# Reading q and the block decays as 32x32 blocks turned by VectorE, and loading v amid a unit's block steps, in a gated linear attention and mixture-of-experts kernel

## The chip, the cores and the metric

The kernel runs on one core of a Trainium2 chip. The metric is device time in microseconds, the median of several runs; lower is better. One further execution was recorded by the hardware profiler.

## The reference

A gated linear attention over 4 batches of 8 heads, 768 tokens and head size 48 is followed by a mixture of 8 experts with a dense, Sinkhorn-normalised routing:

```python
for t in range(S):
    state = alpha[:, :, t, :, None] * state + np.einsum('bhd,bhe->bhde', k[:, :, t], v[:, :, t])
    y[:, :, t] = np.einsum('bhd,bhde->bhe', q[:, :, t], state)
x = y.transpose(0, 2, 1, 3).reshape(3072, 384)
P = np.exp(x @ w_gate - max)
for _ in range(8):
    P /= P.sum(1, keepdims=True) + 1e-9
    P /= P.sum(0, keepdims=True) + 1e-9
    P *= N / E
out = sum(P[:, e:e+1] * (np.maximum(x @ w1[e], 0) @ w2[e]) for e in range(8))
```

## The kernel before, in words

The program has two halves. In the first, up to about 700 us, the attention is computed while TensorE (PE) is filled up with tiles of the first three experts (`moe_tile`; their products stand under the names `ps<-xT,w` and `ps<-w,h`). In the second the other five experts run alone. The change touches the first half only.

The 3072 tokens are cut into 12 units of 256 tokens (4 batches of 3), each of two chunks of 128. Units 0 and 1 go through `direct_chunk`. Units 2 to 11 go through the **block path**. `attn_block` (line 484) works in a layout with a block of 16 tokens of one head on each partition: it loads q, alpha and k into the single-buffered tiles qt, al and kt (line 493), takes products on GpSimd (POOL) and their sums and decays on VectorE (DVE), and at its end writes the decayed k and q, the products of the decays and the block matrix to DRAM scratch (ks, qs, ds, dsw, As; lines 572 to 579). It then reads them back in the token-on-partition layout (KN, QN, DN, an, and VN straight from the input; lines 580 to 587), and reads a window of decays (win, line 592). All of these transfers are issued by SyncE (SP), one after the other, in the order of the code. TAB is 3: from unit 3 on the state uses the table made from win, and k128 is None.

`attn_decays` (line 598) turns the sixteen block decays DN on PE (four transposes into psd, line 604), and DVE copies them to dT. `attn_chunk` (line 641) turns k and q of a chunk on PE: four 128x128 transposes each into psk and psq (line 652), copied to Tk and Tq by ScalarE (ACT, line 654). DVE makes the decayed halves from them (decq, deck). PE then forms psl, psy and the state.

The order of the work is written by hand in the strings START and UNIT (lines 40 and 41): b is a block step, c a chunk step, d the decays, f a piece of an expert tile, a capital lets POOL take the loads. `run` (line 911) obeys them and puts off a step that `early_` holds to be too early. On every engine the instructions then stand in that order, and an instruction that waits holds up all that stands behind it on its engine. An expert tile uses one of four PSUM banks; ACT writes its relu, and DVE the remainder (`h<-ps,h`, line 245), before the bank is free for the fourth tile after it.

```python
for x, y in ((qt, q), (al, alpha), (kt, k)):
    (GE if lop[0] else SP).dma_start(x, src(y))
```

From unit 6 on these three loads are issued by SP right behind the win loads of the unit before; those of units 3 to 5 are issued by POOL.

Of the kernel before, what the change touches and what calls it, by code (L numbers as in the profile page):

```python
# [9 lines left out]
F32 = mybir.dt.float32  # L10
# [15 lines left out]
def tile_gla_moe(ctx: ExitStack, tc: tile.TileContext, q, k, v, alpha, wg, w1, w2, out):  # L26
# [42 lines left out]
    def tr(out_, in_, idn):  # L69
        tc.keep_in_program_order(nc.tensor.transpose(out=out_, in_=in_, identity=idn))  # L70
# [82 lines left out]
    def quarter(j):  # L153
        return slice(32 * j, 32 * j + 32)
# [132 lines left out]

    QN = [ap1.tile([P, NCH, H, DP], F32, name=f"QN{i}") for i in range(2)]
    KN = [ap1.tile([P, NCH, H, DP], F32, name=f"KN{i}") for i in range(2)]
    DN = [ap1.tile([16, H, DP], F32, name="DN")] * 2  # L290
    VW = DP + D
    ST = [ap1.tile([P, NP, 2 * D], F32, name=f"ST{i}") for i in range(2)]
    VN = [ap1.tile([P, NCH, NP, VW], F32, name=f"VN{i}") for i in range(2)]
# [3 lines left out]
    PRE, SUF, Q32, K32 = ([ap1.tile([P, NCH, NP, 2, n], F32, name=f"{x}_{i}") for i in range(2)]  # L297
                          for x, n in (("pre", 4), ("suf", 4), ("q32", 2), ("k32", 2)))

    for x in DN[:1] + ST:  # L300
        GE.memset(x, 0.0)
    for x in PRE + SUF + Q32 + K32:
        GE.memset(x, 1.0)
# [24 lines left out]
    for i in range(NLV):  # L328
        L = 1 << i

        r = sm.tile([P, 16], F32, tag="oddr", name=f"oddr_{i}")
        VE.tensor_reduce(r[:, :16 // L], same.rearrange("p (n z t) -> p n z t", z=2, t=L)[:, :, 0],
                         axis=AX.X, op=ALU.add)
        VE.tensor_copy(odd[:, i].rearrange("p (n t) -> p n t", t=L),
                       r[:, :16 // L].unsqueeze(2).to_broadcast([P, 16 // L, L]))

    def load_v(x, b, t0, Q=SP):
        for r in range(2):
# [145 lines left out]
    def attn_block(b, u, got):  # L484
# [6 lines left out]
        qt, kt, al = (ap1.tile([P, 16, D], F32, tag=x, name=f"{x}_{nm}") for x in ("qt", "kt", "al"))  # L491
        for x, y in ((qt, q), (al, alpha), (kt, k)):
            (GE if lop[0] else SP).dma_start(x, src(y))
        if TAB <= g < TAB + 2:
            SP.dma_start(dsw[g % 2][:, :, 8:].rearrange("h c n d -> (h c) n d"),
                         ones[:2 * H, None, :D].to_broadcast([2 * H, 7, D]))
# [11 lines left out]
        def total(o, t):  # L508
            vec.tensor_reduce(o, t, axis=AX.X, op=ALU.add)
# [35 lines left out]
        if True:  # L545

            t = mult(pool, "tmp4", [16], Af[:, 0:256:17], qt, kt)
            yield
            total(*t)
            yield  # L550
            vec.tensor_mul(qt, qt, al)
            for L in (1, 2, 4, 8):
                todo, merge = level(L)
                for x in todo:
                    t = mult(pool if lop[0] else x[0], *x[1:])
                    yield
                    total(*t)
                    if L == 8:
                        yield
                merge()  # L560
            yield
# [2 lines left out]
        ks = dr.tile([H, U, D], F32, tag="ks", name=f"ks_{nm}")  # L564
        ds = dr.tile([H, 16, D], F32, tag="ds", name=f"ds_{nm}")
        As = dr.tile([H, U, 16], F32, tag="As", name=f"As_{nm}")
        qn, kn, dn = QN[g % 2], KN[g % 2], DN[g % 2]
        vn = VN[g % 2]
        an = ap2.tile([P, NCH, H, 16], F32, tag="an", name=f"an_{nm}")
        def put(t, t_):  # L570
            for x, y in ((ks, ko), (qs, qo)):
                dma(x[:, t:t_].rearrange("h (n t) d -> n h (t d)", t=16), y[t // 2:t_ // 2])

        put(0, U)
        dma(ds.rearrange("h n d -> n h d"), al[:, 0])
        for c in range(NCH) if g >= TAB else ():
            dma(dsw[g % 2][:, c, :8].rearrange("h n d -> n h d"), al[c * 64:c * 64 + 64, 0])
        if True:
            dma(As.rearrange("h (n s) t -> n h (s t)", s=16), Af)
        for c in range(NCH):  # L580
            sl = slice(c * P, (c + 1) * P)
            dma(kn[:, c, :, :D], ks[:, sl].rearrange("h t d -> t h d"))
            dma(qn[:, c, :, :D], qs[:, sl].rearrange("h t d -> t h d"))
            if c == 0:
                dma(dn[:, :, :D], ds.rearrange("h n d -> n h d"))
            dma(an[:, c], As[:, sl].rearrange("h p t -> p h t"))
            load_v(vn[:, c], b, t0 + c * P)
        if g >= TAB:
            win = ap1.tile([P, 7, D], F32, tag="tmp2", name=f"win_{nm}")
# [2 lines left out]
                dma(win[c * 64:c * 64 + 64], bass.AP(tensor=e.tensor, offset=e.offset,  # L592
                                                     ap=[[D, 8], [NCH * 15 * D, H], [1, 7 * D]]))
            got["win"] = win
        got.update(qn=qn, kn=kn, dn=dn, vn=vn, an=an)
        yield

    def attn_decays(b, u, got):

        nm = f"{b}_{u}"  # L600
        dn = got["dn"]
        psd = psa.tile([P, 512], F32, tag="psa", name=f"psd_{nm}")
        for j in range(NP):
            tr(psd[:, j * 16:(j + 1) * 16], dn[:, 2 * j:2 * j + 2].rearrange("p h d -> p (h d)"), ident[:16, :16])
        dT = ap2.tile([P, NCH, NP, 2, 4], F32, tag="dT", name=f"dT_{nm}")
        VE.tensor_copy(dT.rearrange("p c j z n -> p c j (z n)"),
                              psd[:, :NP * 16].rearrange("p (j c n) -> p c j n", c=NCH, n=8))

        g2 = (b * NU + u) % 2
        pre, suf, q32, k32 = PRE[g2], SUF[g2], Q32[g2], K32[g2]  # L610
# [30 lines left out]
    def attn_chunk(b, ch, got):  # L641
# [4 lines left out]
        tt = b * (S // P) + ch  # L646
        nm = f"{b}_{ch}"
        T2 = []
        for s in "kq":
            ps = psa.tile([P, 512], F32, tag="psa", name=f"ps{s}_{nm}")  # L650
            for j in range(NP):
                tr(ps[:, j * P:(j + 1) * P], got[s + "n"][:, c, 2 * j:2 * j + 2].rearrange("p h d -> p (h d)"), ident)
            t = ap2.tile([P, NP, P], F32, tag=f"T{s}", name=f"T{s}_{nm}")
            SE.copy(t.rearrange("p j t -> p (j t)"), ps)
            T2.append(t)
# [18 lines left out]
        for L, tq, tk in ((32, got["q32"][:, c].rearrange("p j z b -> p (j z) b"),  # L674
# [5 lines left out]
        GE.tensor_mul(A.rearrange("p h (n t) -> p n h t", t=16),  # L680
                             got["an"][:, c].unsqueeze(1).to_broadcast([P, 8, H, 16]),
                             mask.unsqueeze(2).unsqueeze(3).to_broadcast([P, 8, H, 16]))
        tabbed = got["k128"] is None
        kb = None
        if tabbed and not c:
            win = got["win"]
# [820 lines left out]
```

## Time and profile before

| | us |
|---|---|
| median of 3 runs (1647.58 to 1651.91) | 1651.86 |
| the profiled execution, its own time | 1645.72 |
| its span, first to last instruction | 1643.8 |
| PE busy | 1591.0 (97%) |
| DVE busy | 1262.3 (77%) |
| ACT busy | 916.5 (56%) |
| POOL busy | 390.9 (24%) |

The busy time of an engine is given with its share of the span. Matmuls are pipelined, so that a busy PE need not be at its peak; what a matmul costs is read from the starts of the instructions that follow each other. The granted TensorE clock was 0.991 of full speed over the span, and full in every stretch from 150 us on that is spoken of below.

### The profile page before, as it was taken

The numbers are of one execution on the slowest core, as the hardware profiler recorded it, in microseconds if no ns is written. First come the engines' busy times: TensorE is split into PE (matmuls) and PEld (weight loads), VectorE is DVE, ScalarE is ACT, GpSimd is POOL, SyncE is SP. The second block draws the span as 40 slices with busy tenths as digits, with TensorE's granted clock in tenths as the row PEclk, the third lists the DMA queues.
The fourth block names the chain that finished last, engine by engine and source line by source line (L and its number), as shares of the span: only waits on it lengthen the run. The fifth ranks groups of instructions, "written<-read, shape, count | busy, mean of one in ns | idle before, by whom it ended". The sixth has DMA issues, their size and how long they took to land.

```text
span 1643.8 us, 50626 instructions
## 1 busy us (share of the span) xinstructions
PE 1591.0 (97%) x21760; PEld 1399.8 (85%) x21760; DVE 1262.3 (77%) x2693; ACT 916.5 (56%) x2106; POOL 390.9 (24%) x395
## 2 busy tenths in 40 slices
PE   5689999999999999999999999999999999999998
PEld 4567777777777777777899999999999999999998
DVE  5887776665666565367798988898888888899998
ACT  3655533333333333355777766666666676765554
POOL 5457544643644462175000000000000000000000
PEclk9799999999999999999999999999999999999999
DMA  7463243144134323120412131213121322213332
GB/s 165 103 139 105 67 116 93 53 125 110 57 89 116 81 69 89 42 79 30 107 50 88 60 98 59 97 60 88 55 92 59 88 69 88 67 62 117 113 121 88
DMA packets 180072, 141.92 MB, mean 86 GB/s; under 512 B 112232, under 2 KB 169832, under 8 KB 179848
## 3 DMA queue, kind: packets, MB, share of 16 engines
q1 hardware_dynamic: 178104, 131.99, 29.0%
q0 software_dynamic: 1744, 6.70, 1.6%
q8 instruction: 170, 2.79, 0.7%
q14 instruction: 54, 0.44, 0.1%
HBM read 91.00 MB, written 47.65 MB: 84 GB/s over the span
## 4 chain that ended last, share of the span: by engine, by line
PE 87%; DVE 4%; DMA 1%; SPq 1%; ACT 1%; issue 1%; POOL 0%; DVEq 0%; ACTq 0%; POOLq 0%
PE ps L67 30%; PE p1a L67 17%; PE p2x L67 14%; PE p1b L67 10%; PE p2y L67 7%; PE p2v L67 4%; PE psl L67 2%; PE psy L67 2%; SPq L58 1%; DVE h L58 1%; DVE w L58 1%; PE psk L70 1%; DVE acc L58 1%; PE psq L70 1%; PE pss L67 0%
## 5 line engine op out<-in xcount | busy, mean ns | idle before, releaser
L67 PEld LDWEIGHTS <-h 128*128 128x128 f16 x6684 | 570.5, 98 | 105.2 <-issue 2.5
L67 PEld LDWEIGHTS <-w 128*128 128x128 f16 x6984 | 565.3, 98 | 58.1 <-issue 12.4
L67 PE MATMUL ps<-xT,w 128*128 128x256 f16 (+1 forms) x2664 | 301.2, 272 | 8.6 <-DVE h L58 6.4
L67 PE MATMUL ps<-w,h 128*128 128x384 f16 x1728 | 299.3, 326 | 0.8 <-DVE h L58 0.7
L58 DVE TENSOR_TENSOR h<-hf,h 128x256 f16<-128x256 f32 x472 | 279.0, 618 | 23.6 <-ACT h L58 23.6
L67 PE MATMUL p2x<-w,h 128*128 128x192 f16 x2820 | 270.7, 246 | 0.0
L58 ACT CAST h<-hf 128x256 f16<-128x256 f32 x472 | 249.5, 567 | 9.3 <-DVE hf L58 4.5
L58 DVE TENSOR_TENSOR hf<-hf 128x256 f32<-128x256 f32 x354 | 181.8, 513 | 39.6 <-ACT hf L58 31.2
L58 ACT ACTIVATE h<-ps 128x256 f16<-128x256 f32 (+1 forms) x296 | 110.5, 377 | 161.5 <-PE ps L67 160.3
L58 POOL TENSOR_TENSOR tmp<-qt,kt 128x768 f32<-128x768 f32 (+2 forms) x87 | 156.2, 1802 | 156.2 <-DVE qt L58 84.6
L58 DVE SCALAR_TENSOR_TENSOR h<-ps,h 128x256 f16<-128x256 f32 (+1 forms) x296 | 117.5, 413 | 96.0 <-ACT h L58 94.7
L67 PE MATMUL p1a<-xT,w 128*128 128x128 f16 (+1 forms) x2160 | 179.1, 237 | 0.0
L67 PE MATMUL p1b<-xT,w 128*128 128x256 f16 (+1 forms) x1440 | 158.0, 246 | 0.0
L58 ACT ACTIVATE hf<-p1b 128x512 f32<-128x512 f32 x118 | 70.3, 596 | 151.4 <-DVE h L58 118.4
L67 PEld LDWEIGHTS <-wx 128*128 128x128 f16 x2160 | 147.4, 98 | 7.9 <-issue 4.9
L67 PE MATMUL p2y<-w,h 128*128 128x192 f16 x1404 | 134.9, 246 | 0.0
L58 DVE TENSOR_REDUCE AB<-tmp 128x16 f32<-128x768 f32 (+2 forms) x90 | 81.4, 904 | 64.1 <-POOL tmp L58 63.7
L67 PE MATMUL p1a<-xc,wx 128*128 128x128 f16 x1440 | 119.5, 219 | 3.6 <-DVE p1b L58 1.6
L58 ACT ACTIVATE hf<-p1a 128x512 f32<-128x512 f32 x118 | 70.4, 597 | 64.7 <-PE p1a L67 64.7
L58 ACT COPY r<-ps 128x384 f32<-128x384 f32 x72 | 34.2, 476 | 102.3 <-PE ps L67 62.3
L58 ACT COPY A<-psl 16x128 f32<-16x128 f32 (+3 forms) x164 | 52.4, 326 | 49.2 <-PE psl L67 47.7
L67 PE MATMUL p2v<-w,h 128*128 128x192 f16 x708 | 68.1, 246 | 0.0
(235 smaller groups left out, 1830.5 us busy)
## 6 DMA issues: line engine op xcount, KB each, us to landing
accd<-acc SPq DMA_DIRECT2D x48, 384.0 KB
acc<-accd SPq DMA_DIRECT2D x48, 384.0 KB
raw<-r SPq DMA_DIRECT2D x72, 192.0 KB
ri<-raw SPq DMA_DIRECT2D x72, 192.0 KB
w1f<-in_moe_w_dram SPq DMA_DIRECT2D x20, 384.0 KB
w2f<-in_moe_w_dram SPq DMA_DIRECT2D x5, 1536.0 KB
VN<-in_v_dram SPq DMA_DIRECT2D x48, 96.0 KB
out_dram<-acc SPq DMA_DIRECT2D x11, 384.0 KB
```

The lines of the kernel that those rows point to most:

```text
L58: r = f(*a, **k_)
L67: tc.keep_in_program_order(nc.tensor.matmul(out_, lhsT, rhs, start=start, stop=stop, **k_))
L70: tc.keep_in_program_order(nc.tensor.transpose(out=out_, in_=in_, identity=idn))
```

## The change

From unit 3 on (`turned`), q and the block decays are written to scratch in two halves by the parity of the head. They are read back in pieces of 32 partitions: rows of 32 and of 16 elements of head size 48 lie one behind the other as 32x32 blocks (four transfers for DY, four for all 256 tokens of QN). One DVE transpose of 32x32 blocks a chunk makes Tq, and one a unit makes dT, in place of the PE transposes and the copies behind them. k is turned on PE as before. The scratch writes begin with ds and dsw. v is loaded in the second block step of the unit where the chunks two units earlier have been recorded far enough (`ahead`), which holds from unit 5 on; units 3 and 4 load it behind an. Unit 2 stays as it was, with DN in a buffer of Tq.

```diff
@@ -287,7 +287,7 @@
 
     QN = [ap1.tile([P, NCH, H, DP], F32, name=f"QN{i}") for i in range(2)]
     KN = [ap1.tile([P, NCH, H, DP], F32, name=f"KN{i}") for i in range(2)]
-    DN = [ap1.tile([16, H, DP], F32, name="DN")] * 2
+    DY = ap1.tile([P, NP * 16 // 32, 32], F32, name="DY")
     VW = DP + D
     ST = [ap1.tile([P, NP, 2 * D], F32, name=f"ST{i}") for i in range(2)]
     VN = [ap1.tile([P, NCH, NP, VW], F32, name=f"VN{i}") for i in range(2)]
@@ -297,7 +297,7 @@
     PRE, SUF, Q32, K32 = ([ap1.tile([P, NCH, NP, 2, n], F32, name=f"{x}_{i}") for i in range(2)]
                           for x, n in (("pre", 4), ("suf", 4), ("q32", 2), ("k32", 2)))
 
-    for x in DN[:1] + ST:
+    for x in [DY] + ST:
         GE.memset(x, 0.0)
     for x in PRE + SUF + Q32 + K32:
         GE.memset(x, 1.0)
@@ -333,6 +333,9 @@
                          axis=AX.X, op=ALU.add)
         VE.tensor_copy(odd[:, i].rearrange("p (n t) -> p n t", t=L),
                        r[:, :16 // L].unsqueeze(2).to_broadcast([P, 16 // L, L]))
+
+    def in32(x):
+        return x.rearrange("p c h d -> p (c h d)").rearrange("p (s t) -> p s t", t=32)
 
     def load_v(x, b, t0, Q=SP):
         for r in range(2):
@@ -491,6 +494,8 @@
         qt, kt, al = (ap1.tile([P, 16, D], F32, tag=x, name=f"{x}_{nm}") for x in ("qt", "kt", "al"))
         for x, y in ((qt, q), (al, alpha), (kt, k)):
             (GE if lop[0] else SP).dma_start(x, src(y))
+        turned = g >= TAB
+        vn = VN[g % 2]
         if TAB <= g < TAB + 2:
             SP.dma_start(dsw[g % 2][:, :, 8:].rearrange("h c n d -> (h c) n d"),
                          ones[:2 * H, None, :D].to_broadcast([2 * H, 7, D]))
@@ -546,6 +551,9 @@
 
             t = mult(pool, "tmp4", [16], Af[:, 0:256:17], qt, kt)
             yield
+            ahead = turned and all(steps[i] >= XDONE[i] for i in range((g - 2) * NCH, (g - 1) * NCH))
+            for c in range(NCH) if ahead else ():
+                load_v(vn[:, c], b, t0 + c * P)
             total(*t)
             yield
             vec.tensor_mul(qt, qt, al)
@@ -564,26 +572,50 @@
         ks = dr.tile([H, U, D], F32, tag="ks", name=f"ks_{nm}")
         ds = dr.tile([H, 16, D], F32, tag="ds", name=f"ds_{nm}")
         As = dr.tile([H, U, 16], F32, tag="As", name=f"As_{nm}")
-        qn, kn, dn = QN[g % 2], KN[g % 2], DN[g % 2]
-        vn = VN[g % 2]
+        qn, kn = QN[g % 2], KN[g % 2]
         an = ap2.tile([P, NCH, H, 16], F32, tag="an", name=f"an_{nm}")
-        def put(t, t_):
+        dsh = lambda: [dma(dsw[g % 2][:, c, :8].rearrange("h n d -> n h d"), al[c * 64:c * 64 + 64, 0])
+                       for c in range(NCH)]
+        load_an = lambda c: dma(an[:, c], As[:, c * P:(c + 1) * P].rearrange("h p t -> p h t"))
+        if turned:
+            heads = lambda x, r: x.rearrange("(r j) t d -> r j t d", r=2)[r]
+            rows = lambda x, r: x.rearrange("(m r) t d -> r m t d", r=2)[r]
+            for r in range(2):
+                dma(heads(ds, r).rearrange("j n d -> n j d"), rows(al, r)[:, 0])
+            dsh()
+            dma(ks.rearrange("h (n t) d -> n h (t d)", t=16), ko)
+            for r in range(2):
+                dma(heads(qs, r).rearrange("j (n t) d -> n j (t d)", t=16), rows(qo, r))
+            dma(As.rearrange("h (n s) t -> n h (s t)", s=16), Af)
+            load_k = lambda c: dma(kn[:, c, :, :D], ks[:, c * P:(c + 1) * P].rearrange("h t d -> t h d"))
+            for x, y in ((DY, ds), (in32(qn), qs)):
+                for i in range(4):
+                    r, z = divmod(i, 2)
+                    w = 32 - 16 * z
+                    dma(x[quarter(i), :, :w], heads(y, r).rearrange("j t d -> (j t) d")
+                        .rearrange("(s t) d -> t s d", t=32)[:, :, 32 * z:32 * z + w])
+                if y is ds:
+                    load_k(0)
+            load_an(0)
+            load_k(1)
+            load_an(1)
+        else:
+            dn = ap2.tile([P, H, DP], F32, tag="Tq", name="DN")[:16]
+            GE.memset(dn[:, :, D:], 0.0)
             for x, y in ((ks, ko), (qs, qo)):
-                dma(x[:, t:t_].rearrange("h (n t) d -> n h (t d)", t=16), y[t // 2:t_ // 2])
-
-        put(0, U)
-        dma(ds.rearrange("h n d -> n h d"), al[:, 0])
-        for c in range(NCH) if g >= TAB else ():
-            dma(dsw[g % 2][:, c, :8].rearrange("h n d -> n h d"), al[c * 64:c * 64 + 64, 0])
-        if True:
+                dma(x.rearrange("h (n t) d -> n h (t d)", t=16), y)
+            dma(ds.rearrange("h n d -> n h d"), al[:, 0])
             dma(As.rearrange("h (n s) t -> n h (s t)", s=16), Af)
-        for c in range(NCH):
-            sl = slice(c * P, (c + 1) * P)
-            dma(kn[:, c, :, :D], ks[:, sl].rearrange("h t d -> t h d"))
-            dma(qn[:, c, :, :D], qs[:, sl].rearrange("h t d -> t h d"))
-            if c == 0:
-                dma(dn[:, :, :D], ds.rearrange("h n d -> n h d"))
-            dma(an[:, c], As[:, sl].rearrange("h p t -> p h t"))
+            for c in range(NCH):
+                sl = slice(c * P, (c + 1) * P)
+                dma(kn[:, c, :, :D], ks[:, sl].rearrange("h t d -> t h d"))
+                dma(qn[:, c, :, :D], qs[:, sl].rearrange("h t d -> t h d"))
+                if c == 0:
+                    dma(dn[:, :, :D], ds.rearrange("h n d -> n h d"))
+                load_an(c)
+                load_v(vn[:, c], b, t0 + c * P)
+            got["dn"] = dn
+        for c in range(NCH) if turned and not ahead else ():
             load_v(vn[:, c], b, t0 + c * P)
         if g >= TAB:
             win = ap1.tile([P, 7, D], F32, tag="tmp2", name=f"win_{nm}")
@@ -592,19 +624,22 @@
                 dma(win[c * 64:c * 64 + 64], bass.AP(tensor=e.tensor, offset=e.offset,
                                                      ap=[[D, 8], [NCH * 15 * D, H], [1, 7 * D]]))
             got["win"] = win
-        got.update(qn=qn, kn=kn, dn=dn, vn=vn, an=an)
+        got.update(qn=qn, kn=kn, vn=vn, an=an)
         yield
 
     def attn_decays(b, u, got):
 
         nm = f"{b}_{u}"
-        dn = got["dn"]
-        psd = psa.tile([P, 512], F32, tag="psa", name=f"psd_{nm}")
-        for j in range(NP):
-            tr(psd[:, j * 16:(j + 1) * 16], dn[:, 2 * j:2 * j + 2].rearrange("p h d -> p (h d)"), ident[:16, :16])
+        dn = got.get("dn")
         dT = ap2.tile([P, NCH, NP, 2, 4], F32, tag="dT", name=f"dT_{nm}")
-        VE.tensor_copy(dT.rearrange("p c j z n -> p c j (z n)"),
-                              psd[:, :NP * 16].rearrange("p (j c n) -> p c j n", c=NCH, n=8))
+        if dn is None:
+            VE.transpose(dT.rearrange("p c j z n -> p j c (z n)"), DY.rearrange("p m (j c n) -> p (m j) c n", c=NCH, n=8))
+        else:
+            psd = psa.tile([P, 512], F32, tag="psa", name=f"psd_{nm}")
+            for j in range(NP):
+                tr(psd[:, j * 16:(j + 1) * 16], dn[:, 2 * j:2 * j + 2].rearrange("p h d -> p (h d)"), ident[:16, :16])
+            VE.tensor_copy(dT.rearrange("p c j z n -> p c j (z n)"),
+                                  psd[:, :NP * 16].rearrange("p (j c n) -> p c j n", c=NCH, n=8))
 
         g2 = (b * NU + u) % 2
         pre, suf, q32, k32 = PRE[g2], SUF[g2], Q32[g2], K32[g2]
@@ -646,7 +681,14 @@
         tt = b * (S // P) + ch
         nm = f"{b}_{ch}"
         T2 = []
+        tabbed = got["k128"] is None
         for s in "kq":
+            if tabbed and s == "q":
+                t = ap2.tile([P, NP, P], F32, tag=f"T{s}", name=f"T{s}_{nm}")
+                y = in32(got["qn"]).rearrange("p (j s) t -> p j (s t)", j=NP)
+                VE.transpose(t, y[:, :, c * P:(c + 1) * P])
+                T2.append(t)
+                continue
             ps = psa.tile([P, 512], F32, tag="psa", name=f"ps{s}_{nm}")
             for j in range(NP):
                 tr(ps[:, j * P:(j + 1) * P], got[s + "n"][:, c, 2 * j:2 * j + 2].rearrange("p h d -> p (h d)"), ident)
@@ -680,7 +722,6 @@
         GE.tensor_mul(A.rearrange("p h (n t) -> p n h t", t=16),
                              got["an"][:, c].unsqueeze(1).to_broadcast([P, 8, H, 16]),
                              mask.unsqueeze(2).unsqueeze(3).to_broadcast([P, 8, H, 16]))
-        tabbed = got["k128"] is None
         kb = None
         if tabbed and not c:
             win = got["win"]
```

The SP queue at the end of the block steps of unit 9, before: the writes, and the reads that follow them.

```order
L58 DMA ks_0_8050<-kt_0_7212 16x8x768
L58 DMA qs_0_8049<-qt_0_7211 16x8x768
L58 DMA ds_0_8051<-al_0_7213 16x8x48
L58 DMA dsw_149<-al_0_7213 8x8x48 x2
L58 DMA As_0_8052<-AB_126 16x8x256
L58 DMA KN_119<-ks_0_8050 128x8x48
L58 DMA QN_117<-qs_0_8049 128x8x48
L58 DMA DN<-ds_0_8051 16x8x48
L58 DMA an_0_8053<-As_0_8052 128x8x16
L58 DMA VN_124<-in_v_dram 128x4x48 x2
```

The same place in the changed program:

```order
L58 DMA ds_0_8009<-al_0_7182 16x4x48 x2
L58 DMA dsw_149<-al_0_7182 8x8x48 x2
L58 DMA ks_0_8008<-kt_0_7181 16x8x768
L58 DMA qs_0_8007<-qt_0_7180 16x4x768 x2
L58 DMA As_0_8010<-AB_126 16x8x256
L58 DMA DY<-ds_0_8009 32x2x32
L58 DMA DY<-ds_0_8009 32x2x16
L58 DMA DY<-ds_0_8009 32x2x32
L58 DMA DY<-ds_0_8009 32x2x16
L58 DMA KN_119<-ks_0_8008 128x8x48
L58 DMA QN_117<-qs_0_8007 32x32x32
L58 DMA QN_117<-qs_0_8007 32x32x16
```

Six issues stood ahead of the first KN read; twelve stand there now. A little further down the same queue, now (before, the four VN issues stood ahead of win):

```order
L58 DMA KN_119<-ks_0_8008 128x8x48
L58 DMA an_0_8011<-As_0_8010 128x8x16
L58 DMA win_0_8032<-dsw_149 64x1x336 x2
L58 DMA qt_1_8035<-in_q_dram 128x1x768
L58 DMA al_1_8037<-in_alpha_dram 128x1x768
L58 DMA kt_1_8036<-in_k_dram 128x1x768
L58 DMA raw_104<-r_14_8074 128x384
L58 DMA raw_104<-r_15_8134 128x384
L58 DMA VN_123<-in_v_dram 128x4x48 x4
```

From the first write to the kt load of the next unit there were 22 issues and are now 25, and VN of the next unit stands behind the two raw writes. On DVE, at the first chunk of unit 9, now:

```order
L58 TENSOR_TENSOR xT_2_84<-ys_5_7990,xT_2_81 128x3x128
L58 STREAM_TRANSPOSE Tq_0_8097<-QN_117 128x512
L58 TENSOR_TENSOR decq_3_0_8099<-Tq_0_8097,q_1_134 128x256
L58 TENSOR_TENSOR deck_3_0_8101<-Tk_0_8095,k_1_136 128x256
L58 TENSOR_TENSOR decq_3_0_8103<-Tq_0_8097,pre_130 128x256
L58 TENSOR_TENSOR win_0_8032<-win_0_8032 128x144
```

The transpose is the one row that is new there; the others stood in the same order before.

## Rows read from the trace of the kernel before

**Rows 1.** Busy time by stage: window and length, then PE, PEld, DVE, ACT, POOL, clock, DMA share, GB/s.

```profile
250.00:308.00 58.00, 58.00 (x770) 44.26 (x768) 39.05 (x79) 21.41 (x59) 30.17 (x23) 1.00 0.35 89
366.00:424.00 58.00, 57.17 (x744) 43.37 (x742) 38.06 (x77) 22.12 (x61) 28.78 (x22) 1.00 0.37 92
```

**Rows 2.** Timeline of PE, decays and first chunk of unit 10: start, duration, instruction.

```profile
573.15 0.42 PE L70 MATMUL psd<-ident,DN 16*128 16x16 f32 x4
573.50 3.10 PE L67 MATMUL ps<-w,h 128*128 128x384 f16 x18
576.44 0.60 PE L70 MATMUL psk<-ident,KN 128*128 128x128 f32 x4
576.88 0.60 PE L70 MATMUL psq<-ident,QN 128*128 128x128 f32 x4
```

**Rows 3.** Timeline of SP's issues at the end of unit 10's block steps.

```profile
560.75 0.58 SPq L58 DMA_DIRECT2D ks<-kt  x1
...
562.07 0.81 SPq L58 DMA_DIRECT2D ds<-al  x1
...
565.48 0.53 SPq L58 DMA_DIRECT2D KN<-ks  x1
...
567.57 1.38 SPq L58 DMA_DIRECT2D an<-As  x1
569.00 1.49 SPq L58 DMA_DIRECT2D VN<-in_v_dram  x2
...
572.77 1.26 SPq L58 DMA_DIRECT2D VN<-in_v_dram  x2
...
576.65 0.59 SPq L58 DMA_DIRECT2D kt<-in_k_dram  x1
```

**Rows 4.** Timelines of PE, POOL and DVE in unit 7's first chunk: idle before, releaser.

```profile
401.62 0.60 PE L70 MATMUL psk<-ident,KN 128*128 128x128 f32 x4
...
409.42 1.80 POOL L58 TENSOR_TENSOR tmp<-qt,kt 128x768 f32<-128x768 f32 x1 [3.79 <-DMA kt<-in_k_dram]
...
412.13 0.41 DVE L58 SCALAR_TENSOR_TENSOR h<-ps,h 128x256 f16<-128x256 f32 x1
...
412.60 1.58 PE L67 MATMUL ps<-xT,w 128*128 128x256 f16 x11 [0.77 <-DVE h L58]
```

**Rows 5.** Timeline of POOL in unit 10's first chunk.

```profile
582.42 1.81 POOL L58 TENSOR_TENSOR tmp<-qt,kt 128x768 f32<-128x768 f32 x1 [1.97 <-DMA kt<-in_k_dram]
```

**Rows 6.** Timelines of SP, POOL, DVE and PE around unit 3's first chunk.

```profile
151.98 0.93 SPq L58 DMA_DIRECT2D ks<-kt  x1
...
157.14 0.54 SPq L58 DMA_DIRECT2D KN<-ks  x1
...
162.49 4.08 SPq L58 DMA_DIRECT2D an<-As  x1
...
152.99 0.28 POOL L58 TENSOR_TENSOR al<-al 128x48 f32<-128x48 f32 x1
...
159.69 0.54 POOL L58 DMA_DIRECT2D qt<-in_q_dram  x1
...
174.07 0.91 DVE L58 TENSOR_TENSOR win<-win 128x144 f32<-128x144 f32 x4 [1.97 <-DMA win<-dsw]
...
178.03 1.14 PE L67 MATMUL ps<-xT,w 128*128 128x256 f16 x9 [1.75 <-DVE h L58]
```

**Rows 7.** Timelines of PE and DVE in unit 4's first chunk.

```profile
233.82 5.07 PE L67 MATMUL ps<-xT,w 128*128 128x256 f16 x45
...
235.97 0.42 DVE L58 SCALAR_TENSOR_TENSOR h<-ps,h 128x256 f16<-128x256 f32 x1
```

**Rows 8.** Timeline of DVE: a whole 128x512 product alone, and a half one beside POOL's.

```profile
614.28 0.68 DVE L58 TENSOR_TENSOR Tq<-Tq,q 128x512 f32<-128x512 f32 x1
...
578.62 2.11 DVE L58 TENSOR_TENSOR deck<-Tk,k 128x256 f32<-128x256 f32 x1
```

**Rows 9.** DMA queues from 571 to 575 us: packets, MB, share of 16 engines.

```profile
q1 hardware_dynamic: 4572, 0.73, 103.0%
```

## The prediction

> **What bounds the kernel now.** I read the busy time by stage first. From 250 us to the end of the attention TensorE is busy in all 58.00 us of a stage of one unit, or in 57.17 of them, at the full clock [rows 1], while VectorE is busy for 39 and GpSimd for 30. So whatever leaves PE shortens the kernel, as long as nothing else is as long as PE. The second view is therefore the timeline of one unit: how far behind PE is the block path, whose chain is closed in itself (write to scratch, read back, load the next q, alpha and k, compute, write)? The answer is that it is hardly behind. In unit 7 the product that waits for kt starts 7.80 us after the first transpose of k (409.42 less 401.62), VectorE is then late for a PSUM bank, and PE stands idle for 0.77 us [rows 4]. So a start up to 7.80 - 0.77 = 7.03 us after that transpose is free. In unit 10 it is 5.98 us (582.42 less 576.44) and costs nothing [rows 2, 5]: the slack there is 1.05 us. I take 0.5 us as the mean slack of the six units (5 to 10) whose tail loads q, alpha and k for the next unit, between 0 and 1.05. This is the number on which the forecast turns: PE is full, but a second loop of nearly the same length runs beside it.
>
> **What PE loses.** Four transposes of q take from 576.44 to 576.88 by the twin case of k, so 0.44 us [rows 2]; 18 chunks (units 3 to 11, two each) make 7.9 us. Four transposes of the decays take from 573.15 to 573.50, 0.35 us [rows 2]; nine units make 3.2 us. Sum: 11.1 us. One row says that a transpose lasts long: four of them cover 0.60 us, and their starts are still only 0.11 us apart, since they overlap [rows 2]. The Trainium skill (TensorE: Matmul & The Clock Gate, Part 4: PE-mode transpose) gives about 275 ns for one 128x128 transpose in a kernel, which it puts down to access latency. By that figure the 72 transposes of q alone would be an estimated 19.8 us; the starts in the trace decide against it, because latency that overlaps is not paid again.
>
> ScalarE loses 18 copies of 128x512; it is busy for 22 of 58 us [rows 1] and gives nothing to the end. VectorE gains 18 transposes of 128x512. No such row exists before. The nearest is a product of the same size, 0.68 us alone; the upper end is 2.11 us, which a half-sized product took beside GpSimd's work [rows 8]; below nothing it cannot be. I take 0.68, 12 us over 18 chunks, and put it at nothing in the sum: VectorE has 19 us free in a unit [rows 1], and at the first chunk it no longer waits for ScalarE's copy of q. If that cover were gone the first to notice would be the h remainders behind decq, which hold PSUM banks. The small dT transpose replaces a small copy, and is taken as equal.
>
> **What SyncE gains.** From the first scratch write to the kt load there are 25 issues where there were 22. The second ds half costs 0.81 us and a gap, 0.85. Six more of the others (one qs, three DY, two QN) I price as the KN read, 0.53 us and a gap of 0.1: 3.8 us. The four VN issues that move away gave 1.49 + 1.26 us and two gaps, 2.85. The first an read took 1.38 us [rows 3]; I count half, 0.7, as waiting for the block matrix, which by then will have landed. So kt is issued 0.85 + 3.8 - 2.85 - 0.7 = 1.1 us later. Ends: if an issue to 32 partitions cost a quarter of one to 128, the result is 1.7 us earlier; if all six cost what ds costs and the an wait stays, 3.2 us later. I take 1.1, since DY and QN are three-dimensional as KN is. The VN loads behind the raw writes stand after kt, so they do not delay it; they delay td and kb by some 2.5 us, which are needed a chunk later.
>
> In units 5 to 10 the product behind kt then comes 1.1 us later, and PE arrives 0.44 + 0.35 = 0.79 us earlier. Less 0.5 of slack, PE waits 1.4 us, and six units give back 8.3 us. The loads behind win are not hidden by anything else on POOL or VectorE, which stand in line behind the product.
>
> **The two early units.** Units 3 and 4 have both evils. Their VN loads stay in the burst, and the next q, alpha and k are loaded by GpSimd's queue at a fixed place in the middle of it: from 159.69 us in unit 3, after which SyncE's next issues crawl (4.08 us for one an) [rows 6]. Before, the KN and QN reads get away ahead of that: KN is issued 5.2 us after the first write (157.14 less 151.98). Now the first write is ds, which needs al, and in unit 3 al is done at 153.27, 1.3 us later [rows 6]; and twelve issues stand ahead of KN in place of six, about 4 us more (0.85 for the ds half, five at 0.63). So KN, the doubled packets of QN, an and win all fall into the crowded stretch. QN alone brings 2048 more packets a unit; 4572 small packets kept the queues full for 4 us [rows 9], so they are worth up to 1.8 us. I take win as 4 us later, between 1 (only some packets' worth) and 5.5 (the whole delay of KN in unit 3 passed on).
>
> What is behind it: in unit 3 VectorE already waits 1.97 us for win, and PE 1.75 for the h behind it [rows 6], so there is no slack: 4 + 0.79, 4.8 us. In unit 4 PE's five tiles start at 233.82 and 1.0 us apart; the fifth in line for the bank needs the first h, done at 236.39, by about 236.8 [rows 7]. The slack is 0.4: 4.4 us. Together 9.2 us, between 3.2 and 12.2.
>
> **The sum.** -11.1 + 8.3 + 9.2 = +6.4 us. The profiled execution took 1645.7 us (span 1643.8), so it becomes 1652.1; the median of the runs shown is 1651.9, 6.2 above it, so for the median I say 1658.3 us. A difference under 0.3% (5 us) I count as none, since that is about the scatter of the runs.
>
> **The rivals.**
> *The gain stays.* If the new issues are cheap, or the scratch reads land before they are needed, the chain keeps its length and PE's 11.1 us come through, less the 3.2 us of the early units' lower end: about 1644 us. For it: PE is busy for 58.00 of 58.00 us, and the tail of the burst loses four VN reads. Against: a chain that had a slack of 1.05 us at most cannot shrink by 1.2 us a unit unless kt comes earlier, and nothing in the change makes it so. Chance 0.25. The skill's figure for a transpose would lead to this side as well: by it, the estimate for PE's gain is 19.8 + 3.2 us, and the sum is 5.5 us faster, near 1646. The starts in the trace leave that a chance of 0.02 at most, held in the 0.25.
> *Half of it.* Only one of the two losses comes: with the early units alone, -11.1 + 9.2 = -1.9; with the six later ones alone, -2.8. The time is 1649 to 1650 us, no difference that can be measured. For it: each loss hangs on one estimate, the price of an issue or the crowding of the queues. Chance 0.25.
> *VectorE becomes the bound.* If a transpose costs 2.11 us, the second chunk of a unit, where the transpose stands right behind a sum and ahead of decq, makes the h remainders late. It decides once VectorE is later by the about 1 us of slack that a unit has, and gives up to 1.1 us more for nine units, 10 us on top of the sum: 1668. Chance 0.05, a part of slower.
> *The change does not take hold.* If v were still loaded in the burst, kt would be another 2.85 us later. The recorded order shows v behind the raw writes from unit 5 on, so this is left out.
>
> **How the numbers follow.** Slower by over 0.3% holds my forecast and the VectorE case, 0.50; within 0.3%, 0.25; faster, 0.25. The range goes from the first rival's time less the 0.77 us for which PE stood in unit 7 [rows 4], 1643, to the dear end of both losses short of the extreme: kt later by 2 us (six times 2.3, 13.7) and the early units' 12.2, which is +14.8, 1667 us. The likeliest case's own range is 1655 to 1664.
>
> **What would show it.** In the changed profile psq should be left only in unit 2, psd once. PE should wait for DVE's h in units 5 to 10, about 1.4 us each, behind POOL's product that waits for the kt load; the kt issue should end about 1 us later after the first write. In units 3 and 4 the wait for win or QN on DVE should be some 4 us longer, and PE idle there by about 9 us in all. I am wrong if SyncE reaches kt as early as before, if PE's stages of a unit stay full at 56.8 us instead of 58, or if DVE's transposes take over 1 us.

## The result and the profile after

The changed kernel took 1665.42 us (median of four runs, 1661.41 to 1667.53), the kernel before beside it 1651.53 us (1647.58 to 1651.91). The ratio is 1.0087, with a 95% interval of 1.0061 to 1.0112: 14 us slower, of which the forecast had 6.4. The median lies within the stated range (1643 to 1667 us), 1.4 us above the likeliest case's own (1655 to 1664). The profiled execution took 1661.41 us, its span is 1659.7.

The page gives the busy time of each engine over the span.

```profile
PE 1588.9 (96%) x21652; PEld 1394.8 (84%) x21652; DVE 1276.5 (77%) x2711; ACT 907.9 (55%) x2088; POOL 390.7 (24%) x396
```

PE is busy for 2 us less, not 11, at a mean granted clock of 0.977 in place of 0.991; the span is 15.9 us longer, so PE stands idle for 18 us more. The stages tell where. The columns are those of [rows 1]; in the changed kernel the first two lines are units 3 and 4, and the last two answer to [rows 1]:

```profile
150.00:200.00 50.00, 43.62 (x581) 33.01 (x580) 34.38 (x68) 22.16 (x56) 26.71 (x22) 0.93 0.46 102
200.00:250.00 50.00, 42.94 (x540) 32.58 (x539) 30.43 (x63) 15.65 (x45) 18.25 (x17) 0.96 0.47 103
250.00:308.00 58.00, 58.00 (x765) 43.90 (x764) 38.62 (x78) 20.59 (x58) 27.19 (x21) 0.98 0.36 87
366.00:424.00 58.00, 56.34 (x735) 42.61 (x734) 38.85 (x76) 21.14 (x59) 29.35 (x21) 1.00 0.39 95
```

The kernel before, units 3 and 4:

```profile
150.00:200.00 50.00, 48.25 (x629) 37.97 (x628) 36.71 (x72) 25.16 (x63) 28.50 (x24) 1.00 0.43 103
200.00:250.00 50.00, 49.09 (x684) 36.39 (x682) 37.31 (x72) 19.03 (x54) 23.48 (x22) 1.00 0.43 103
```

The waits of PE in the changed kernel from 150 to 656 us (total, times, longest) tell for whom:

```profile
PE ps L67 <- DVE h L58: 23.3, 11, 6.4
```

Of 23.3 us in 11 waits, 9.8 us in eight lie after 250 us (units 5 to 10); the two of units 3 and 4 are 6.4 us each. Before, the same view had 3.2 us in three waits. All are for VectorE's h: the remainder that frees a PSUM bank.

**A later unit.** SyncE's issues in unit 10, which answer to [rows 3], then PE, POOL and DVE there, which answer to [rows 2, 5]:

```profile
575.37 1.21 SPq L58 DMA_DIRECT2D ds<-al  x2
...
591.89 0.59 SPq L58 DMA_DIRECT2D kt<-in_k_dram  x1
```

```profile
590.54 0.60 PE L70 MATMUL psk<-ident,KN 128*128 128x128 f32 x4
...
590.01 0.71 DVE L58 STREAM_TRANSPOSE Tq<-QN 128x512 f32<-128x512 f32 x1 [0.57 <-DMA QN<-qs]
...
598.51 1.81 POOL L58 TENSOR_TENSOR tmp<-qt,kt 128x768 f32<-128x768 f32 x1 [3.78 <-DMA kt<-in_k_dram]
...
600.36 0.95 DVE L58 TENSOR_REDUCE AB<-tmp 128x16 f32<-128x768 f32 x1 [3.09 <-POOL tmp L58]
601.23 0.41 DVE L58 SCALAR_TENSOR_TENSOR h<-ps,h 128x256 f16<-128x256 f32 x1
...
601.69 1.14 PE L67 MATMUL ps<-xT,w 128*128 128x256 f16 x9 [1.37 <-DVE h L58]
```

kt's issue ends 17.1 us after the first write (592.48 less 575.37; before 16.5), and POOL's product starts 23.1 us after it (before 21.7). Of that delay 0.6 us is the issue's and 0.85 the load's own time, 6.03 us where it was 5.18; why the load took longer, no run shows. VectorE stands behind the product, h behind VectorE's sum, and PE idles for 1.37 us. In unit 7 [rows 4] it idles for 1.15 us, before for 0.77.

**Unit 3**, SyncE, DVE and PE, answering to [rows 6]:

```profile
154.02 1.72 SPq L58 DMA_DIRECT2D ds<-al  x2
...
162.57 4.55 SPq L58 DMA_DIRECT2D QN<-qs  x4
167.16 4.85 SPq L58 DMA_DIRECT2D an<-As  x1
...
173.37 3.13 SPq L58 DMA_DIRECT2D VN<-in_v_dram  x4
176.56 1.30 SPq L58 DMA_DIRECT2D win<-dsw  x2
...
173.44 0.71 DVE L58 STREAM_TRANSPOSE Tq<-QN 128x512 f32<-128x512 f32 x1 [4.76 <-DMA QN<-qs]
...
179.88 0.91 DVE L58 TENSOR_TENSOR win<-win 128x144 f32<-128x144 f32 x4 [1.57 <-DMA win<-dsw]
...
183.84 2.08 PE L67 MATMUL ps<-xT,w 128*128 128x256 f16 x9 [6.38 <-DVE h L58]
```

**Unit 4**, POOL, DVE and PE, answering to [rows 7]:

```profile
230.67 0.54 POOL L58 DMA_DIRECT2D qt<-in_q_dram  x1 [3.42 <-DMA DY<-ds]
...
240.23 1.81 POOL L58 TENSOR_TENSOR tmp<-qt,kt 128x768 f32<-128x768 f32 x1 [7.55 <-DMA kt<-in_k_dram]
...
242.58 1.89 POOL L58 TENSOR_TENSOR A<-an,mask 128x1024 f32<-128x1024 f32 x1
...
242.07 0.95 DVE L58 TENSOR_REDUCE AB<-tmp 128x16 f32<-128x768 f32 x1 [7.22 <-POOL tmp L58]
242.94 0.70 DVE L58 STREAM_TRANSPOSE Tq<-QN 128x512 f32<-128x512 f32 x1
...
246.66 0.92 DVE L58 TENSOR_TENSOR win<-win 128x144 f32<-128x144 f32 x4 [1.24 <-DMA win<-dsw]
...
248.95 3.88 PE L67 MATMUL ps<-xT,w 128*128 128x256 f16 x18 [6.36 <-DVE h L58]
```

In unit 3 VectorE waits for QN, then for win. In unit 4 it is held first by POOL's product, whose kt load was itself issued late: POOL waited 3.42 us before it could load qt, 10.0 us after the first write (220.69); before, the load went out 7.2 us after it, without a wait. The product then starts 19.5 us after the first write, where it was 15.9. The kernel before, SyncE's first write and POOL in unit 4:

```profile
213.07 0.58 SPq L58 DMA_DIRECT2D ks<-kt  x1
...
220.25 0.55 POOL L58 DMA_DIRECT2D qt<-in_q_dram  x1
...
229.00 1.81 POOL L58 TENSOR_TENSOR tmp<-qt,kt 128x768 f32<-128x768 f32 x1 [7.16 <-DMA kt<-in_k_dram]
```

qt, al and kt have one buffer each, which is free for the load only when the scratch writes have read it, and the writes of k and q now come later. The row names DY's read as what POOL waited for; experiment 5 shows that it was the writes. After each of the two idle times PE starts at half its clock, the 1.2 GHz level (windows, columns as in [rows 1]):

```profile
180.90:187.70 6.80, 3.86 (x119) 2.91 (x120) 6.43 (x13) 0.75 (x2) 4.21 (x3) 0.50 0.21 64
245.80:252.60 6.80, 3.65 (x18) 2.46 (x17) 5.46 (x14) 0.38 (x1) 3.51 (x4) 0.50 0.53 145
```

PE works for 3.86 and 3.65 us in these windows at half speed, so about 3.7 us of its work are lost (an estimate from these two rows); the nine matmuls at 183.84 take 2.08 us, where [rows 6] has 1.14.

### The profile page after: what moved, and what is told of

It reads as the page before. It is cut to its first block, busy times and chain, and to the rows that moved or that the text cites. A ratio compares the mean times of both kernels' runs of the same rounds, so it can differ in the third digit from the quotient of the medians.

```text
span 1659.7 us, 50492 instructions
## 1 busy us (share of the span) xinstructions
PE 1588.9 (96%) x21652; PEld 1394.8 (84%) x21652; DVE 1276.5 (77%) x2711; ACT 907.9 (55%) x2088; POOL 390.7 (24%) x396
## 4 chain that ended last, share of the span: by engine, by line
PE 80%; DVE 8%; SPq 4%; DMA 3%; POOL 2%; issue 2%; ACT 1%; DVEq 0%; POOLq 0%; ACTq 0%
PE ps L67 24%; PE p1a L67 16%; PE p2x L67 14%; PE p1b L67 9%; PE p2y L67 7%; SPq L58 4%; PE p2v L67 4%; DMA kt<-in_k_dram 2%; PE psl L67 2%; POOL tmp L58 2%; PE psy L67 2%; DVE AB L58 1%; DVE T L58 1%; DVE w L58 1%; DVE h L58 1%
## 5 line engine op out<-in xcount | busy, mean ns | idle before, releaser
L67 PE MATMUL ps<-xT,w 128*128 128x256 f16 (+1 forms) x2664 | 305.6, 274 | 27.7 <-DVE h L58 25.5
L58 DVE TENSOR_TENSOR h<-hf,h 128x256 f16<-128x256 f32 x472 | 279.0, 618 | 23.6 <-ACT h L58 23.6
```

The source lines that it names most:

```text
L58: r = f(*a, **k_)
L67: tc.keep_in_program_order(nc.tensor.matmul(out_, lhsT, rhs, start=start, stop=stop, **k_))
```

## The experiments

Each kernel ran beside the kernel before on the same chip, and each ratio is against that. "Idle" is PE's longest idle time before h in unit 3 and in unit 4, in us; "waits" is all its waiting for h from 250 to 656 us, in us and times. It includes unit 4 where the matmul behind that wait starts after 250.

| | ratio (95%) | idle in units 3, 4 | waits |
|---|---|---|---|
| the kernel before | 1 | 1.8, 0 | 0.8 in 1 |
| the change | 1.0087 (1.0061 to 1.0112) | 6.4, 6.4 | 9.8 in 8 |
| 1: units 5 to 11 alone | 1.0031 (1.0019 to 1.0044) | 1.0, 1.0 | 11.5 in 8 |
| 2: units 3 and 4 alone | 1.0074 (1.0062 to 1.0086) | 7.6, 5.4 | 6.8 in 3 |
| 3: PE's work alone | 0.9977 (0.9969 to 0.9986) | 2.8, 0.9 | 4.5 in 6 |
| 4: v in the burst | 1.0244 (1.0231 to 1.0257) | 8.2, 7.7 | 33.4 in 7 |
| 5: old order of writes | 1.0077 (1.0061 to 1.0093) | 6.7, 0 | 10.4 in 7 |
| 6: early loads on SyncE | 1.0105 (1.0082 to 1.0127) | 6.7, 6.2 | 18.6 in 9 |
| 7: kt earlier | 1.0028 (1.0015 to 1.0041) | 7.0, 6.8 | 3.2 in 5 |
| 8: kt earlier, before | 0.9998 (0.9985 to 1.0011) | 1.8, 0 | 0.8 in 3 |
| 9: win first in 3, 4 | 1.0099 (1.0084 to 1.0114) | 4.8, 4.9 | 17.4 in 9 |
| 10: all reordered | 0.9991 (0.9979 to 1.0003) | 2.9, 4.4 | 0.4 in 2 |
| 11: late turned, reordered | 0.9941 (0.9927 to 0.9955) | 1.0, 0 | 1.8 in 4 |
| 12: early read as before, reordered | 0.9927 (0.9913 to 0.9941) | 0, 0 | 1.6 in 4 |

**1 and 2. Which units.** The change in units 5 to 11 alone, and in units 3 and 4 alone; DN has its own buffer again. The other units write and read as before the change.

```diff
-        turned = g >= TAB
+        turned = g >= TAB + 2          # 1
+        turned = TAB <= g < TAB + 2    # 2
```

> Turned reads from unit 5 on; units 3 and 4 as before. Theory A (the two early units make the loss: by the starts of the first transpose of k, the changed kernel falls behind by 11.3 us from unit 3 to unit 5 and by 2.5 us over units 5 to 11): +2.5 us against before, 0 to +4, and no idle time of PE above 2 us at units 3 and 4. Theory B (the later kt of units 5 to 10 makes it): +12 us or more. Theory C (the loss is spread, TensorE's clock or DMA traffic everywhere): some +10 us.

> Turned reads in units 3 and 4 alone, with their writes and reads as in the change; units 5 to 11 as before. Theory A: +11 us against before, 8 to 14, with two idle times of PE of about 6.4 us and the granted clock down behind each. Theory B: within 2 us of before, since PE even loses 2.5 us of work. Theory C: +3 us.

The early units alone cost 12.2 us (0.0074 of 1648.8), the late ones alone 5.1 us (3.1 to 7.3). Theory A holds for the early ones, with idle times of 7.6 and 5.4 us; the late ones cost twice what it said, and more than its 0 to 4 us. Together the parts make 17 us, the change 14, a difference within the intervals.

**3. PE's work alone.**

```diff
         for s in "kq":
+            if got["k128"] is None and s == "q":
+                t = ap2.tile([P, NP, P], F32, tag=f"T{s}", name=f"T{s}_{nm}")
+                SE.copy(t.rearrange("p j t -> p (j t)"), ps)
+                T2.append(t)
+                continue
...
+        off = b * NU + u >= TAB
+        psd = ones if off else psa.tile([P, 512], F32, tag="psa", name=f"psd_{nm}")
+        for j in range(0 if off else NP):
```

> The kernel before, without the transposes of q and of the decays on PE from unit 3 on; all transfers as before. Left out: the turning of q (Tq is copied from the bank of the turned k) and the decays (a constant takes their place). PE loses 11.1 us by my rows. If PE alone were the bound: -11 us. If the block path closes right behind PE with 0.5 us of slack in units 5 to 10, as I took it: -0.5 us in each of the six, and at most 1.2 us in units 3, 4 and 11, together -3 to -7 us.

3.8 us came of 11.1, with all transfers as before, and PE's waits after 250 us rose from 0.8 to 4.5 us. The idle times of units 3 and 4 rose too, by 2.0 us together, and the clock from 150 to 200 us was 0.97. The block path takes back most of what PE loses.

**4. v in the burst.**

```diff
-            ahead = turned and all(
+            ahead = False and all(
```

> The changed kernel with v loaded in the burst, ahead of win and of the next unit's loads, in all units. If kt's issue decides in units 5 to 10: kt is issued 2.8 us later (four issues), PE's wait for h in each of the six units grows by as much, +17 us against the changed kernel, 10 to 20. If something else made those waits: within 3 us of the changed kernel.

26 us over the change (0.0157 of 1648.8), beyond the range. PE's waits rose by 23.6 us, of which 7.7 are unit 4's, now behind 250 us, so by 15.9 us in units 5 to 10: that is near the 17 forecast. Units 3 and 4 idle 3.1 us longer. The rest, some 7 us, stands beside a clock of 0.94 to 0.97 in each stage of 58 us from 250 to 656, where the change has 0.98 in the first and 1.00 in the others; that the clock is its cause is not tested.

**5. The old order of writes.** ks and qs first, then ds and dsw.

> The changed kernel with ks and qs written first, as before, and ds and dsw behind them. If the late start of the ks and qs writes is what makes POOL's q and k loads and the QN reads late in units 3 and 4: these loads start 2 to 3 us earlier after the first write, PE's two idle times fall from 6.4 us to about 4, -3 to -6 us against the changed kernel. If it is the number of reads in the crowded stretch: within 2 us of it. In units 5 to 10 nothing is expected, since kt's issue stands where it stood.

By the time it is the second theory's case: 1.6 us lower, within the intervals. By unit 4's rows (SyncE, POOL, DVE) it is the first's:

```profile
223.49 0.57 SPq L58 DMA_DIRECT2D ks<-kt  x1
...
228.81 3.31 SPq L58 DMA_DIRECT2D DY<-ds  x4
...
230.76 0.55 POOL L58 DMA_DIRECT2D qt<-in_q_dram  x1
...
240.25 0.95 DVE L58 TENSOR_REDUCE AB<-tmp 128x16 f32<-128x768 f32 x1 [1.82 <-POOL tmp L58]
```

POOL's load goes out 7.3 us after the first write, without a wait and while SyncE is still issuing DY's reads, and VectorE waits 1.82 us for the product in place of 7.22. So it was the late scratch writes, not DY's reads, that held the load back in the change. PE's idle time before h is gone in unit 4, but PE waits 2.4 us there for KN, and unit 3 stays at 6.7 us: so the time hardly moves.

**6. POOL's loads of units 4 and 5 on SyncE.** Here and below `fetch_in(g, x)` issues the load of q or k of unit g on SyncE; the place where it stood then leaves it out.

```diff
             load_an(0)
+            if g in (3, 4):
+                fetch_in(g + 1, "q")
+                fetch_in(g + 1, "k")
             load_k(1)
```

> The changed kernel, with q and k of units 4 and 5 loaded by SyncE behind the first an read of the units before, in place of POOL's queue (alpha stays there). If the crowding of POOL's 128-row loads with SyncE's reads makes the loss in units 3 and 4: QN lands 2 to 3 us earlier, PE's idle times fall from 6.4 us each to 2 to 3, the clock stays full, -6 to -9 us against the changed kernel. If it is the traffic as a whole, wherever it is issued: within 2 us. If kt becomes late instead: PE waits behind the product of q and k, 0 to -3 us.

No gain: 1.0105 beside 1.0087, with intervals that overlap. SyncE, DVE and PE in unit 3 show why:

```profile
171.97 5.98 SPq L58 DMA_DIRECT2D VN<-in_v_dram  x4
...
178.00 1.27 SPq L58 DMA_DIRECT2D win<-dsw  x2
...
170.62 0.71 DVE L58 STREAM_TRANSPOSE Tq<-QN 128x512 f32<-128x512 f32 x1 [1.64 <-DMA QN<-qs]
...
181.37 0.91 DVE L58 TENSOR_TENSOR win<-win 128x144 f32<-128x144 f32 x4 [7.14 <-DMA win<-dsw]
...
185.33 2.08 PE L67 MATMUL ps<-xT,w 128*128 128x256 f16 x9 [6.73 <-DVE h L58]
```

VectorE waits 1.64 us for QN in place of 4.76, as the crowding theory has it, but then 7.14 us for win, which stands behind v. One cause went, and the other filled its place. In unit 4 it still waits 7.15 us for the product.

**7 and 8. kt earlier**, in the changed kernel and in the one before (there behind the first chunk's v).

```diff
             load_an(0)
+            if g >= 5:
+                fetch_in(g + 1, "q")
+                fetch_in(g + 1, "k")
             load_k(1)
```

> The changed kernel, with q and k of units 6 to 11 loaded behind the first an read of the unit before, ahead of the second chunk's reads and win. kt is issued some 4 us earlier after the first write. If PE's waits in units 5 to 10 are kt's (9.8 us of idle time in the changed kernel's trace): they go but for what win or the second chunk's reads make late instead, -7 to -10 us against the changed kernel. If VectorE's transposes or the reads of QN make them: within 2 us.

> The kernel before with the same order of loads in units 5 to 10 (q and k of the next unit behind the first chunk's v). If the block path there closes just behind PE, PE has 0.8 us of idle time to lose and then is the bound: 0 to -2 us against before. If the path itself set the pace of the units: 1 us a unit and more, -6 us or more.

Both as forecast by the theory of a path that closes just behind PE: 9.7 us off the change (1.0087 to 1.0028), nothing off the kernel before. PE's waits after 250 us fall from 9.8 to 3.2 us.

**9 and 10. Both causes.** Number 9 puts win behind the first an read in units 3 and 4, with POOL's loads as they are; number 10 puts qt, kt and then win there, in all units from 3 on.

```diff
             load_an(0)
+            if g in (3, 4):            # 9
+                load_win()
...
+            fetch_in(g + 1, "q")       # 10
+            fetch_in(g + 1, "k")
+            load_win()
             load_k(1)
```

> The changed kernel with the win loads of units 3 and 4 issued behind the first an read, ahead of the second chunk's reads and of v; POOL's loads as they are. If win behind the four v loads is what holds VectorE, and PE behind it, in both units: win lands 4 to 5 us earlier, PE's idle times fall from 6.4 us to 2 to 3, -6 to -9 us against the changed kernel. If each unit has a second cause of nearly the same length (QN in unit 3, POOL's late load of k in unit 4, by the waits of 4.8 us for QN and 7.6 us for kt in its trace): an idle time falls by the win wait alone, 1.6 and 1.2 us, -2 to -4 us. If it is the traffic as a whole: within 2 us.

> The changed kernel with both causes met in all units from 3 on: behind the first an read come q and k of the next unit, then win, then the second chunk's reads and v. If two causes of nearly the same length hold units 3 and 4, one falls only with the other: PE's idle times there fall to 3 us or less, -6 to -9 us on top of the 10 us that the earlier k gave units 5 to 10, so -15 to -18 us against the changed kernel and 0 to -4 us against before. If the early loss is traffic: -8 to -11 us against the changed kernel, some +4 us against before.

Number 9's idle times fell by 1.6 and 1.4 us, about the waits for win. Its time, forecast 2 to 4 us lower, came out 2.0 us higher, within the intervals. In its execution unit 3's first write came 2.5 us later (156.52 and 154.02), ahead of all that the edit touches, and the waits of units 5 to 10 were 2.7 us longer (17.4 less unit 4's 4.9, against 9.8); that these ate the gain is not shown. Its DVE, in units 3 and 4:

```profile
175.62 0.71 DVE L58 STREAM_TRANSPOSE Tq<-QN 128x512 f32<-128x512 f32 x1 [4.43 <-DMA QN<-qs]
...
180.76 0.90 DVE L58 TENSOR_TENSOR win<-win 128x144 f32<-128x144 f32 x4
...
245.01 0.95 DVE L58 TENSOR_REDUCE AB<-tmp 128x16 f32<-128x768 f32 x1 [7.11 <-POOL tmp L58]
```

No wait for win is left, and QN and kt hold VectorE. In number 10 the idle times fall to 2.9 and 4.4 us, where 3 or less were forecast for each, and the time is 15.8 us under the change's, as expected; 9.7 of that is number 7's. For unit 3 this shows two causes, of which one falls only with the other. In unit 4 the second is not met: POOL's product, here its row, starts 18.9 us after the first write (221.24), where the change had 19.5, and VectorE still waits 6.62 us for it.

```profile
240.18 1.81 POOL L58 TENSOR_TENSOR tmp<-qt,kt 128x768 f32<-128x768 f32 x1 [11.90 <-DMA kt<-in_k_dram]
```

**11 and 12. What is left.** Number 11 is number 1 with number 10's order in units 5 to 11. Number 12 gives that order to units 3 and 4 as well, which read q the old way.

```diff
                 load_an(c)
+                if not c and g >= TAB:
+                    fetch_in(g + 1, "q")
+                    fetch_in(g + 1, "k")
+                    load_win()
                 load_v(vn[:, c], b, t0 + c * P)
```

> Units 3 and 4 as before the change; units 5 to 11 turned, with q and k of the next unit and win behind the first an read in them. If the block path alone kept PE's gain from the end: seven units give back all of PE's part, 14 times 0.44 and seven times 0.35 us, -8.6 us against before, -7 to -9. If some of the gain is lost to VectorE's transposes or to the DMA queues: -2 to -5.

> As the run beside it (units 5 to 11 turned and reordered), and units 3 and 4, read in the old way, also get q and k of the next unit and win behind the first an read, in place of POOL's loads. If it is the new writes and the 32-block reads that leave PE 2.9 and 4.4 us of idle time in units 3 and 4 even in the new order: these fall under 2 us each here, and the time is 0 to -2 us against the run beside it. If it is the new place of the loads that costs there: idle times of 3 us and more, +2 to +5 us.

Number 11 is 9.7 us faster than before (interval 7.4 to 12.0 us): PE's whole part of 8.6. In its unit 10 kt's issue ends 13.8 us after the first write (555.50), and the product starts 20.2 us after it, where the change had 17.1 and 23.1:

```profile
568.70 0.60 SPq L58 DMA_DIRECT2D kt<-in_k_dram  x1
...
575.68 1.81 POOL L58 TENSOR_TENSOR tmp<-qt,kt 128x768 f32<-128x768 f32 x1 [0.82 <-DMA kt<-in_k_dram]
```

Number 12 is the fastest, 1637.55 us beside 1649.49 and 2.5 us under number 11 (forecast 0 to 2, and the intervals overlap), with no idle time left in units 3 and 4: SyncE's and DVE's rows of its unit 3 have win early, and no wait for it.

```profile
162.93 1.24 SPq L58 DMA_DIRECT2D win<-dsw  x2
...
173.88 0.90 DVE L58 TENSOR_TENSOR win<-win 128x144 f32<-128x144 f32 x4
```

So it is the turned reading of units 3 and 4, with its new writes and 32-block reads, and not the new place of the loads, that leaves number 10 its 2.9 and 4.4 us. In unit 4 one way is seen: with the new writes and reads ahead of it, kt's issue ends 14.0 us after the first write in number 10, and 9.8 us after it in number 12. The shares of the later writes, of QN's doubled packets and of PE's earlier arrival were not taken apart.

## Why the prediction was right, and where it was too small

**The turning point held.** The forecast rested on the block path running just behind PE. Experiment 3 (3.8 us of 11.1), 7 (9.7 us from an earlier kt) and 8 (nothing without PE's gain) show it. In unit 10 the product came 7.97 us after the first transpose of k, and PE idled 1.37 us, so a start up to 6.60 us would have been free. The prediction read 7.03 us from unit 7, with four transposes of q in between that PE no longer has (0.44): that makes 6.59. Units 6, 7 and 9 give 6.60, 6.59 and 6.61 in the same way, units 5 and 8 only 5.73 and 5.62.

**PE's part.** 11.1 us for nine units is 8.6 for seven; experiment 11 gave 9.7, interval 7.4 to 12.0; the earlier kt by itself gave nothing before (experiment 8). The starts in the trace were the right price. The Trainium skill (TensorE: Matmul & The Clock Gate, Part 4: PE-mode transpose) has about 275 ns for a 128x128 transpose. By that figure, an estimate, the seven units would be 15.4 us for q, to which the starts add 2.5 for the decays; the run does not agree.

**kt.** I said 1.1 us later by its issue. The issue ends 0.6 us later in unit 10, and the load takes 0.85 us longer: near in size, wrong in its parts, which is luck. (The dear end of this delay, 3.2 us, comes to 3.1 by its terms.) The six waits of PE were 8.3 us in the sum; in the trace the first chunks of the six units have 8.4, from 0.39 to 2.57 us each, and the second chunks of units 9 and 10 another 1.4, together 9.0 more than before (9.8 less 0.8). But experiment 1 puts the late units' whole effect at +5.1 us, where my terms give -0.3 (8.3 less 8.6). Its trace has 11.5 us of waits and a stage at a clock of 0.97. The late term was low, by 1 to 5 us according to the execution.

**The early units: the term that was mis-sized.** I said 9.2 us. Experiment 2's 12.2 us and the 2.5 us of PE's work that they lose make 14.7. In the change's own trace 4.6 and 6.4 us of added idle time and 3.7 of clock come to the same; in experiment 2's trace the added idle time is 11.3 us. In unit 3 the step was right: win, 22.1 us after the first write before (174.07 less 151.98), came 25.9 us after it (179.88 less 154.02), 3.8 us later where I took 4; PE's idle time rose by 4.6, forecast 4.8. In unit 4 I gave 4.4 us for win, and it was 6.4. There h came 4.9 us later after the first write where I took 4: 3.6 by the product and 1.2 by win. And PE came 1.9 us earlier against that write where I took 0.79 (with its first transpose of k at 233.01 less 220.69, before 226.88 less 213.07, and four transposes of q fewer). Less the slack of 0.4, that is the 6.4. The sentence that failed is that GpSimd's queue loads q, alpha and k "at a fixed place in the middle" of the burst. The place is fixed in POOL's order, but the load waits for its buffer, and so for the scratch writes, which the change puts later (experiment 5); VectorE was then held by the product. And I priced nothing for the clock: 3.7 us. That the total still lies within the range is partly luck: this term went past its own dear end of 12.2 us, and the late waits stayed below theirs of 13.7.

**The rest.** VectorE as the bound did not come: 18 transposes of 0.70 us each, against 0.68 in the sum, and experiment 11 has PE's gain whole with 14 of them. In unit 10 the h remainders of the second chunk start 18.73 us after the first chunk's product in both kernels (617.24 less 598.51; before 601.15 less 582.42): the transpose lengthened nothing there. The gain that stays, and half of it, fell with the early units. Most of what was to be seen was seen: psq only in unit 2, psd once, PE's waits in units 5 to 10, transposes under 1 us. But kt's issue ended 0.6 us later, not 1, unit 4's wait on DVE was for the product, and PE's idle time in the early units was 12.7 us, not 9.

## What to carry to other kernels

Before work is taken from a full engine, measure how far behind it the next loop runs: here it ran so close that 11 us of removed work were worth 4 (experiment 3). When transfers are put later, follow each single-buffered tile that they read to the load that waits for it, also on another queue. Where an engine stands behind two late transfers, mending one may show nothing in the time (experiments 6 and 9): look whether its wait went, and mend both before judging.

## What was not expected of the hardware

The clock fell behind some short idle times of PE. In number 10 the two were 2.9 and 4.4 us, and these are the windows from PE's restart (columns as in [rows 1]):

```profile
183.30:190.00 6.70, 6.68 (x137) 5.12 (x137) 5.40 (x13) 3.52 (x11) 5.81 (x5) 0.54 0.18 61
...
247.50:254.00 6.50, 6.42 (x142) 4.92 (x142) 5.58 (x12) 2.19 (x6) 4.96 (x5) 0.74 0.10 36
```

The length of the idle time alone does not decide it. Of these two the shorter brought the lower clock. And here is PE in unit 6 of experiment 1, then in unit 5 of experiment 9:

```profile
358.39 3.49 PE L67 MATMUL ps<-xT,w 128*128 128x256 f16 x18 [2.28 <-DVE h L58]
...
314.47 2.13 PE L67 MATMUL ps<-xT,w 128*128 128x256 f16 x18 [3.15 <-DVE h L58]
```

The same 18 matmuls take 3.49 us behind 2.28 us of idle time (granted clock 0.61 from 358.4 to 361 us) and 2.13 us behind 3.15 (1.00 from 314.5 to 318). What else decides it, no run here takes apart.

The transposes were not slowed by POOL, where VectorE's products were. Beside POOL's A at 242.58 the changed kernel's transpose took 0.70 us, as elsewhere (18 of them below: minimum, median and maximum in ns), while half-sized decq products, second line, ran from 0.42 to 1.76 us:

```profile
L58 DVE STREAM_TRANSPOSE Tq<-QN x18: 695/703/712, 173.4 to 662.9; 128x512 f32<-128x512 f32 x18
...
L58 DVE TENSOR_TENSOR decq<-Tq,q x20: 424/460/1762, 113.9 to 663.7; 128x256 f32<-128x256 f32 x20
```

The Trainium skill (GPSIMD Engine Reference, 1. Specifications) says that GpSimd's SBUF interfaces are shared with VectorE, with contention by VectorE's instructions that have two SBUF inputs, among others. The rows agree: the product has two such inputs, the transpose one. By it the upper end of 2.11 us could have been left out of the forecast.
